# Full-precision array pieces for the attention's scores, the gate and z, and the first expert unit started after one sequence

## The chip, the cores and the metric

The kernel runs on one core of one Trainium2 chip. Its engines are TensorE (PE, with its weight loads shown as PEld), VectorE (DVE), ScalarE (ACT), GpSimd (POOL) and SyncE (SP, which issues the loads). Each works through its own queue in order. The metric is the device time of one execution in microseconds; the time of a kernel is the median of its runs.

## What is computed

Three networks follow one another (B = 4 sequences, 8 heads, 576 tokens, 64 columns a head, 32 packed keys; 2304 tokens of 512 columns in all):

```python
p_packed = sm_attn(p, k, v)                 # 32 packed queries against 576 keys, softmax
x = sm_attn(q, p_packed, p_packed)          # 576 queries against the 32 packed keys
P = exp(x @ w_gate - max)                   # 8 experts, then 8 rounds of row and column scaling
out = sum_e P[:, e] * (relu(x @ w1[e]) @ w2[e])       # w1: 512 x 1024, w2: 1024 x 512
h = relu(out @ w_in); y = (s * h * h + b) @ w_out     # 512 x 2048, 2048 x 512
```

All of it is float32. The large products are made of three products of rounded parts: high with high, high with low, low with high (`PASSES`), in the type fp32r. A product of two float32 tiles without such parts is called full precision here; the trace shows it as two instructions.

## The kernel before, in words

**The second attention is never multiplied by its values.** The experts read the weights of the second softmax instead (`xa`, heads x packed keys in 256 rows, high and low part), and the packed values are multiplied into w1: for each unit and pair of sequences, z = packed values x w1 (`zmm`, L340). A unit is 256 hidden columns of one expert; there are 32. Each unit goes over two pairs of sequences, a pair in four blocks of 288 tokens: `mm1a` (L373) multiplies z and xa, takes the relu on ACT (L381) and the residue on DVE (L382); `tile2` (L385) multiplies by w2 and `put1` (L394) adds to the sums of all tokens in `acc`, with the gate's factor `pm` from the fifth unit on.

**z before.** `zmm` makes four batches per unit (n = 0 to 3), each four fp32r matmuls over 128 rows that hold the high and low parts of two heads' values against w1's own high and low parts. w1 is loaded twice, into rows 0-63 and 64-127 (`load_w1`, L80), rounded on ACT (L88), and its residue made on POOL (L89). Since the values of four sequences stand side by side in 32-row blocks, `zput` (L355) takes a batch apart with six copies on ACT (L369) and six residues on DVE (L371).

**The attention before** goes in eight groups of four heads. The first scores (`s1`, L161) and the second ones (`s2`, L223) are full-precision matmuls on 64 columns of the array with zeros for the head that isn't meant (L167, L232); the values (`av`, L195) use 32 columns. A group goes through eleven stages, each a number of waves after its first (`STAGES`, L264; `wave`, L267), so several groups are under way. All eleven waves up to L522 are issued before the first `mm1a`; the remaining stages of the last groups run beside the four blocks of unit 0's first pair (L525 to L531).

**The order is written out by hand.** A block is a `slot` (L449): two `mm1a`, and between and behind them the `tile2` that earlier blocks made ready, each followed by one side job. `side1` (L479) gives the side jobs of the experts: one z batch at a time for the next unit, the loads of w1 and w2. From the second pair of unit 0 on each block also takes one step of `balance` (L273): the gate's products, then eight rounds of scaling (L320 to L335), each of a row part on DVE, one matmul with ones (L327) and a column part on DVE. It has 20 steps and is emptied after the first block of unit 3 (L549), ahead of the first use of `pm`.

**Buffers.** PSUM holds three banks for `tile2` (ps_y), two for `mm1a` (ps_h), three for all else (ps_m). Keys, values and first weights of the attention lie in `acc`, which the experts reach later. Loads are issued by SP in program order.

Of the kernel before, what the change touches and what calls it, by code (L numbers as in the profile page):

```python
# [30 lines left out]
KC, NKC = 96, 6      # keys of a chunk, chunks  # L31
SCALE = 1.0 / 8.0    # 1 / sqrt(HD)
# [5 lines left out]
def tile_kernel(ctx: ExitStack, tc: tile.TileContext, qT, kT, vv, pb, w1c, w2c, wcat64, wg, sv, bv, out):  # L38
# [20 lines left out]
    wgr = const.tile([128, NC, E], F32, name="wgr")  # L59
# [8 lines left out]

    def x_part(n, c):
        return xa[n][:, c, :] if c < 2 else xb[n][:, c - 2, :]  # L70

# [1 line left out]
    wts = {}  # L73
    tmp_p = []
# [5 lines left out]
    def load_w1(u):  # L80
        # a head's rows: high parts in rows 0-63, low parts in rows 64-127
        w = w_new((1, u))
        for i in range(2):
            r = raw_p.tile([128, 1024], F32, tag="raw", name="raw")
            for n in range(2):
                nc.sync.dma_start(out=r[64 * n:64 * n + 64, :], in_=w1c[u, :, 1024 * i:1024 * i + 1024])
            yield
            A.copy(w[:, i, :], r)  # L88
            G.tensor_tensor(out=w[64:128, i, :], in0=r[64:128, :], in1=w[64:128, i, :].bitcast(F32),  # L89
                            op=ALU.subtract)  # L90
# [9 lines left out]
    def load_w64(key, f):  # L100
        # float64 words to float32: (mantissa + 2^20) * (sign, exponent - 20), rounded to nearest
# [26 lines left out]
    NG = B * 2  # L128
    at = {}

# [3 lines left out]
    accf = acc.rearrange("p t d -> p (t d)")  # L134

    def spare(o, n):
        # rows of acc, which the experts reach after the attention
        return accf[:, o:o + n]

    def a_load(g):  # L140
        b, i = divmod(g, 2)
        if i == 0:
            pbs[b] = at_p.tile([128, NC, 2 * NPK], F32, tag="pbs", bufs=2, name="pbs")
            nc.sync.dma_start(out=pbs[b], in_=pb[:, b])
        k_ = spare(2 * S * (g % 3), 2 * S).rearrange("p (j t) -> p j t", j=2)
        nc.sync.dma_start(out=k_, in_=kT[b, :, 2 * i:2 * i + 2, :])
        at[g] = {"k": k_}

    def a_loadv(g):
        b, i = divmod(g, 2)  # L150
        v_ = spare(8 * S + NKC * 256 * (g % 2), NKC * 256)[:KC].rearrange("p (c m) -> p c m", c=NKC)
        nc.sync.dma_start(out=v_, in_=vv[b, :, :, 256 * i:256 * i + 256])
        at[g]["v"] = v_

    def a_loadq(g):
        b, i = divmod(g, 2)
        q_ = at_p.tile([128, 2, S], F32, tag="q", bufs=2, name="q_")
        nc.sync.dma_start(out=q_, in_=qT[b, :, 2 * i:2 * i + 2, :])
        at[g]["q"] = q_

    def s1(g):  # L161
        b, i = divmod(g, 2)
        k_, st = at[g].pop("k"), at_p.tile([128, 8], F32, tag="st", bufs=4, name="st")
        ps = [psa("y", "ps_s") for _ in range(2)]
        for hh in range(2):
            for j in range(2):
                mmul(ps[hh][64 * j:64 * j + 64, :HB], pbs[b][:, 2 * i + j, :],  # L167
                     k_[:, j, hh * HB:(hh + 1) * HB], start=True, stop=True)
            V.tensor_reduce(out=st[:, hh:hh + 1], in_=ps[hh][:, :HB], axis=AX.X, op=ALU.max)
        V.tensor_scalar(out=st[:, 2:3], in0=st[:, 0:1], scalar1=st[:, 1:2], scalar2=-SCALE,  # L170
                        op0=ALU.max, op1=ALU.mult)
        at[g]["st"], at[g]["s1"] = st, ps

    def exp1(g):
        st, ps, a1 = at[g]["st"], at[g].pop("s1"), spare(S * (6 + g % 2), S)
        for hh in range(2):
            A.activation(out=a1[:, hh * HB:(hh + 1) * HB], in_=ps[hh][:, :HB], func=AF.Exp,
                         bias=st[:, 2:3], scale=SCALE, accum_out=st[:, 3 + hh:4 + hh])
        V.tensor_scalar(out=st[:, 5:6], in0=st[:, 3:4], scalar1=st[:, 4:5], scalar2=EPS,
                        op0=ALU.add, op1=ALU.add)  # L180
        V.reciprocal(out=st[:, 6:7], in_=st[:, 5:6])
        at[g]["a1"] = a1

    def a1t(g):
        a1 = at[g].pop("a1")
        aT = at_p.tile([KC, NKC, 128], F32, tag="aT", bufs=2, name="aT")
        for hh in range(2):
            p_ = psa("m", "ps_t")
# [4 lines left out]
        at[g]["aT"] = aT  # L193

    def av(g):  # L195
        aT, v_, st = at[g].pop("aT"), at[g].pop("v"), at[g].pop("st")
        p_ = psa("m", "ps_v")
        for c in range(NKC):
            for n in range(4):
                r = slice(32 * n, 32 * n + 32)  # L200
                mmul(p_[r, :HD], aT[:, c, r], v_[:, c, HD * n:HD * n + HD], start=(c == 0), stop=(c == NKC - 1))
        w = at_p.tile([128, 2, HD], F32, tag="xw", bufs=2, name="xw")
        i_ = p_[:, :HD].rearrange("p (a d) -> p a d", a=1).to_broadcast([128, 2, HD])
        A.activation(out=w, in_=i_, func=AF.Copy, scale=st[:, 6:7])
        at[g]["w"] = w

    def ppt(g):
        # a head's packed values, transposed, in rows 0-63 and again in rows 64-127
        b, i = divmod(g, 2)
        p_ = psa("h", "ps_p")  # L210
        nc.tensor.transpose(p_[:, :128], at[g].pop("w").rearrange("p a d -> p (a d)"), ident)
        pv = p_[:, :128].rearrange("p (c j n) -> p c j n", c=2, j=2)
        for j in range(2):
            r, o = slice(64 * j, 64 * j + 64), NPK * (j ^ (b & 1))
            A.copy(ppf[r, b, 2 * i:2 * i + 2, o:o + NPK], pv[r, :, j, :])
        s_ = [p_[:, NPK * n:NPK * n + NPK] for n in range(4)]
        o = [[pp[:, i, n, k, b ^ n, :] for n in range(4)] for k in range(2)]
        for n in range(4):
            A.copy(o[0][n], s_[n])  # L219
        for n in range(4):  # L220
            V.tensor_tensor(out=o[1][n], in0=s_[n], in1=o[0][n].bitcast(F32), op=ALU.subtract)

    def s2(g):  # L223
        b, i = divmod(g, 2)
        q_ = at[g].pop("q")
        s_ = at_p.tile([128, S // 32, 32], F32, tag="s2", bufs=3, name="s2")
        st = at_p.tile([128, 4, S // 32, 1], F32, tag="st2", bufs=4, name="st2")
        for hh in range(2):
            p_ = psa("yh"[hh], "ps_q")
            for j in range(2):  # L230
                o = 64 * (j ^ (b >> 1))
                mmul(p_[o:o + 64, :HB], ppf[:, b, 2 * i + j, :], q_[:, j, hh * HB:(hh + 1) * HB],  # L232
                     start=True, stop=True)
            V.transpose(out=s_[:, 9 * hh:9 * hh + 9, :].rearrange("p t m -> p (t m)"), in_=p_[:, :HB])
        V.tensor_reduce(out=st[:, 0, :, 0], in_=s_, axis=AX.X, op=ALU.max)
        at[g]["s2"], at[g]["st2"] = s_, st

    def sub2(g):
        s_, st = at[g]["s2"], at[g]["st2"]
        G.tensor_tensor(out=s_, in0=s_, in1=st[:, 0].to_broadcast([128, S // 32, 32]), op=ALU.subtract)  # L240

    def exp2(g):
        A.activation(out=at[g]["s2"], in_=at[g]["s2"], func=AF.Exp, scale=SCALE)

    def norm2(g):
# [109 lines left out]
    def zput(u, n, p_, prs=(0, 1)):  # L355
# [3 lines left out]
        for q in range(4):  # L359
            r, pr = slice(32 * q, 32 * q + 32), (q >> 1) ^ k  # L360
            if pr not in prs:
                continue
# [257 lines left out]
```

## Time and profile before

| | us |
|---|---|
| median of 3 runs | 1840.36 |
| lowest, highest | 1840.31, 1841.12 |
| the profiled execution: its span | 1839.9 |
| PE, DVE, ACT, POOL busy in it | 1761.9, 1399.3, 809.2, 410.1 |

The profile is of one execution. Its span runs from the first to the last instruction; the median stands 0.4 us above it. "Lnnn" is a line of the kernel before. A row of the timeline has its start, how long it lasted from the first to the last end, engine, line, operation, the tiles (out <- in), its shape and count; what is in brackets is idle time of the engine ahead of it and what ended it. Consecutive instructions of one line are merged, and the end of a matmul includes its way through the array, so the start of the next row is the better mark of where a group's work was over. A row of the stage windows gives busy time (and instructions) per engine in that stretch, the mean granted clock of TensorE as a share of 2.4 GHz, the DMA engines' busy share, and what they moved.

### The profile page before, as it was taken

The numbers are of one execution on the slowest core, as the hardware profiler recorded it, in microseconds if no ns is written. First come the engines' busy times: TensorE is split into PE (matmuls) and PEld (weight loads), VectorE is DVE, ScalarE is ACT, GpSimd is POOL, SyncE is SP. The second block draws the span as 40 slices with busy tenths as digits, with TensorE's granted clock in tenths as the row PEclk, the third lists the DMA queues.
The fourth block names the chain that finished last, engine by engine and source line by source line (L and its number), as shares of the span: only waits on it lengthen the run. The fifth ranks groups of instructions, "written<-read, shape, count | busy, mean of one in ns | idle before, by whom it ended". The sixth has DMA issues, their size and how long they took to land.

```text
span 1839.9 us, 26426 instructions
## 1 busy us (share of the span) xinstructions
PE 1761.9 (96%) x9797; PEld 1519.7 (83%) x9797; DVE 1399.3 (76%) x2828; ACT 809.2 (44%) x1845; POOL 410.1 (22%) x288
## 2 busy tenths in 40 slices
PE   5789999999999999999999999999999999999999
PEld 2478888888888888888888888888888978888888
DVE  2757978777777777777777787777999489888874
ACT  3574475445444444544444454444434422222222
POOL 2541112111112211111221111121112233333332
PEclk9799999999999999999999999999999999999999
DMA  9421111111111111111111111111011011111102
GB/s 247 131 58 46 35 36 49 44 35 35 46 35 35 56 37 35 35 46 35 35 58 35 35 35 46 35 35 58 24 35 46 12 35 46 47 35 35 35 12 103
DMA packets 30225, 88.23 MB, mean 48 GB/s; under 512 B 4240, under 2 KB 9360, under 8 KB 30096
## 3 DMA queue, kind: packets, MB, share of 16 engines
q1 hardware_dynamic: 30096, 86.54, 16.2%
q8 instruction: 77, 1.26, 0.3%
q14 instruction: 52, 0.43, 0.1%
HBM read 81.81 MB, written 4.72 MB: 47 GB/s over the span
## 4 chain that ended last, share of the span: by engine, by line
PE 63%; DVE 20%; ACT 6%; issue 5%; POOL 2%; DMA 2%; SPq 0%; ACTq 0%; POOLq 0%; DVEq 0%
PE ps L390 37%; PE ps L378 18%; DVE z L371 6%; ACT z L369 5%; PE ps L415 5%; PE ps_z L351 2%; DVE m L120 2%; DVE ex L114 2%; DVE acc L403 1%; POOL h L425 1%; DVE m L119 1%; DVE acc L432 1%; DVE g L422 1%; DVE ex L116 1%; DVE ex L111 1%
## 5 line engine op out<-in xcount | busy, mean ns | idle before, releaser
L390 PE MATMUL ps<-w,h 128*128 128x512 f32 x4320 | 1119.3, 396 | 33.8 <-ACT h L424 9.4
L390 PEld LDWEIGHTS ps<-w,h 128*128 128x128 f32 x4320 | 778.5, 188 | 200.9 <-DVE h L382 19.9
L378 PEld LDWEIGHTS ps<-xa,z 128*128 128x128 f32 x3072 | 465.4, 189 | 46.6 <-ACT z L369 3.4
L378 PE MATMUL ps<-xa,z 128*128 128x288 f32 x3072 | 495.9, 297 | 4.9 <-ACT z L369 3.0
L403 DVE SCALAR_TENSOR_TENSOR acc<-ps,pm,acc 128x512 f32<-128x512 f32 x504 | 374.1, 747 | 109.3 <-PE ps L390 107.9
L381 ACT ACTIVATE h<-ps 128x288 fp32r<-128x288 f32 x512 | 210.7, 411 | 555.8 <-PE ps L378 502.3
L371 DVE TENSOR_TENSOR z<-ps_z,z 32x256 fp32r<-32x256 f32 (+1 forms) x768 | 370.3, 506 | 39.3 <-ACT z L369 33.8
L382 DVE SCALAR_TENSOR_TENSOR h<-ps,h 128x288 fp32r<-128x288 f32 x512 | 232.6, 454 | 128.1 <-ACT h L381 121.3
L369 ACT CAST z<-ps_z 32x256 fp32r<-32x256 f32 (+1 forms) x768 | 310.2, 434 | 18.2 <-PE ps_z L351 7.2
L89 POOL TENSOR_TENSOR w<-raw,w 64x1024 fp32r<-64x1024 f32 x64 | 152.6, 2405 | 414.9 <-issue 378.7
L98 POOL TENSOR_TENSOR w<-raw,w 128x1024 fp32r<-128x1024 f32 x32 | 76.9, 2402 | 596.4 <-ACT w L97 560.2
L425 POOL TENSOR_TENSOR h<-g,h 128x384 fp32r<-128x384 f32 x96 | 100.9, 1051 | 249.2 <-ACT h L424 247.2
L415 PE MATMUL ps<-xa,w 128*128 128x384 f32 x576 | 147.5, 337 | 0.0
L415 PE MATMUL ps<-xb,w 128*128 128x384 f32 x576 | 147.1, 336 | 0.0
L424 ACT CAST h<-g 128x384 fp32r<-128x384 f32 x96 | 49.4, 514 | 161.2 <-DVE g L423 161.1
L422 DVE SCALAR_TENSOR_TENSOR g<-ps,r 128x384 f32<-128x384 f32 x96 | 53.0, 552 | 77.1 <-ACT r L421 75.7
L415 PEld LDWEIGHTS ps<-xa,w 128*128 128x128 f32 x576 | 105.6, 188 | 6.7
L415 PEld LDWEIGHTS ps<-xb,w 128*128 128x128 f32 x576 | 104.7, 188 | 0.0
L88 ACT CAST w<-raw 128x1024 fp32r<-128x1024 f32 x64 | 67.0, 1047 | 67.1 <-PE ps L390 63.0
L432 DVE TENSOR_TENSOR acc<-ps,acc 128x512 f32<-128x512 f32 x126 | 86.0, 684 | 9.2 <-PE ps L390 9.0
L351 PE MATMUL ps_z<-w,pp 128*128 128x256 f32 x512 | 82.4, 283 | 0.7 <-ACT pp L219 0.5
L124 POOL TENSOR_TENSOR w<-m,w 128x256 fp32r<-128x256 f32 x64 | 48.1, 751 | 127.0 <-ACT w L123 127.0
(108 smaller groups left out, 776.9 us busy)
## 6 DMA issues: line engine op xcount, KB each, us to landing
raw<-w1c SPq DMA_DIRECT2D x128, 256.0 KB, 3.9
raw<-w2c SPq DMA_DIRECT2D x32, 512.0 KB, 3.4
raw<-wcat SPq DMA_DIRECT2D x32, 512.0 KB, 3.4
acc<-kT SPq DMA_DIRECT2D x8, 576.0 KB, 9.6
acc<-vv SPq DMA_DIRECT2D x8, 576.0 KB, 10.5
out<-acc SPq DMA_DIRECT2D x18, 256.0 KB, 2.0
q__224<-qT SPq DMA_DIRECT2D x1, 576.0 KB, 10.2
q__299<-qT SPq DMA_DIRECT2D x1, 576.0 KB, 14.8
```

What stands on the lines that cost most here:

```text
L89: G.tensor_tensor(out=w[64:128, i, :], in0=r[64:128, :], in1=w[64:128, i, :].bitcast(F32), op=ALU.subtract)
L351: mmul(p_[:, j * FU:(j + 1) * FU], pp[:, i, m, a].rearrange("p q n -> p (q n)"), w[:, (4 * i + m) * FU:(4 * i + m + 1) * FU], start=(a == ...
L369: A.copy(o[:, 0], i_)
L371: V.tensor_tensor(out=o[:, 1], in0=i_, in1=o[:, 0].bitcast(F32), op=ALU.subtract)
L378: mmul(p_[:, :HB], z[:, a, q // 2, i, f * 128:(f + 1) * 128], xa[k][:, i, t], start=(n + i == 0), stop=(n + i == 3))
L381: A.activation(out=hh, in_=p_[:, :HB], func=AF.Relu)
L382: V.scalar_tensor_tensor(out=hl, in0=p_[:, :HB], scalar=0.0, in1=hh.bitcast(F32), op0=ALU.max, op1=ALU.subtract)
L390: mmul(y, h[:, f, a, hc:hc + 128], ws[f][k], start=(n == 0), stop=(n == 3 * UF - 1))
L403: V.scalar_tensor_tensor(out=a, in0=y, scalar=pm[:, T, u // UE:u // UE + 1], in1=a, op0=ALU.mult, op1=ALU.add)
L415: mmul(p, w[:, a, c * 128:(c + 1) * 128], x_part(k, c)[:, b * BLK:(b + 1) * BLK], start=(n == 0), stop=(n == 3 * NC - 1))
L425: G.tensor_tensor(out=hl, in0=g, in1=hh.bitcast(F32), op=ALU.subtract)
L432: V.tensor_tensor(out=a, in0=y, in1=a, op=ALU.add)
```

## The change

Scores, gate and z become full-precision matmuls on pieces of 64 rows and 32 columns of the array, one piece a head, eight heads at a time. `heads()` names the piece of a head: row half r, column quarter c. Two PSUM banks, one for each row half, take the results.

- z: one job per unit and pair of sequences, 16 matmuls of 256 columns, then per bank one copy on ACT and one residue on DVE over 128 rows. w1 is loaded once, as it is; there is no rounding and no residue of it.
- Packed values stay in one layout (`ppf`); the zero blocks and the rounded copies go.
- The attention goes by sequence. The first runs alone up to its `xa`, with its subtractions and products on DVE; the next one's scores and exponentials follow. Then unit 0 begins: two blocks for each sequence, the next sequence's attention as their side jobs. From the third block on, in the first block of a sequence, the `tile2` go ahead of the `mm1a` (`behind`).
- `slot` spreads many side jobs over the block instead of one per job and the rest at the end.
- The gate's steps begin with unit 1 and are emptied where they were.
- w1 is loaded some one and a half units ahead. PSUM: ps_y 2, ps_h 2, ps_m 4. z has three buffers instead of four.

```diff
-    z_p = pool("z", 4)
-    ps_y = pool("ps_y", 3, space=bass.MemoryType.PSUM)
+    z_p = pool("z", 3)
+    ps_y = pool("ps_y", 2, space=bass.MemoryType.PSUM)
...
-    ps_m = pool("ps_m", 3, space=bass.MemoryType.PSUM)
+    ps_m = pool("ps_m", 4, space=bass.MemoryType.PSUM)
...
+    def heads():
+        for c in range(4):
+            for r in range(2):
+                yield r, c, slice(64 * r, 64 * r + 64), slice(32 * c, 32 * c + 32)
...
     def load_w1(u):
...
+        w = wts[1, u] = w1_p[-1].tile([128, 4, FU], F32, tag="w1", name="w1_")
+        wv = w1c[u].rearrange("d (c r m) -> r d c m", c=4, r=2)
+        for r in range(2):
+            nc.sync.dma_start(out=w[64 * r:64 * r + 64], in_=wv[r])
...
+    def s1(b, hh, tags="mm"):
+        ps = [psa(t, "ps_s") for t in tags]
+        for r, c, rows, cols in heads():
+            mmul(ps[r][cols, :HB], pbs[rows, b, c, NPK * r:NPK * r + NPK],
+                 at["k", b, c // 2][rows, c % 2, hh * HB:(hh + 1) * HB], start=True, stop=True)
+        at["s1", b, hh] = ps
...
+    def ppt(b, tag="m"):
+        p_ = psa(tag, "ps_p")
+        nc.tensor.transpose(p_[:, :128], at.pop(("w", b)).rearrange("p r d -> p (r d)"), ident)
+        A.copy(ppf[:, b, :], p_[:, :128])
...
+    def s2(b, hh, tags="mm"):
+        ps = at["s2p", b, hh] = [psa(t, "ps_q") for t in tags]
+        for r, c, rows, cols in heads():
+            mmul(ps[r][cols, :HB], ppf[rows, b, cols],
+                 at["q", b, c // 2][rows, c % 2, hh * HB:(hh + 1) * HB], start=True, stop=True)
...
+    def zmm(u, pr, qs=(0, 1)):
+        w = wts[1, u]
+        ps = [psm("ps_z") for _ in range(2)]
+        for q in qs:
+            for r, c, rows, cols in heads():
+                mmul(ps[r][cols, q * FU:(q + 1) * FU], ppf[rows, 2 * pr + q, cols], w[rows, c, :],
+                     start=True, stop=True)
+        return ps
+
+    def zput(u, pr, ps, qs=(0, 1)):
...
+        for r in range(2):
+            i_ = ps[r].rearrange("p (q m) -> p q m", q=2)[:, qs[0]:qs[-1] + 1]
+            A.copy(z[:, 0, qs[0]:qs[-1] + 1, r, :], i_)
+            V.tensor_tensor(out=z[:, 1, qs[0]:qs[-1] + 1, r, :], in0=i_,
+                            in1=z[:, 0, qs[0]:qs[-1] + 1, r, :].bitcast(F32), op=ALU.subtract)
...
-    def slot(first, side=()):
+    def slot(first, side=(), behind=False):
...
-        per = [first[0]] + todo[:1] + [first[1]] + todo[1:]
+        per = todo + first if behind else [first[0]] + todo[:1] + [first[1]] + todo[1:]
+        done = 0
         for n, job in enumerate(per):
             job()
-            if side:
-                side.pop(0)()
-        for s_ in side:
+            upto = max(min(n + 1, len(side)), len(side) * (n + 1) // len(per))
+            while done < upto:
+                side[done]()
+                done += 1
+        for s_ in side[done:]:
             s_()
...
     def side1(x, q):
         jobs = []
+        u, pr = order[x]
+        if u + 1 < U1 and (pr, q) in ((0, 2), (1, 0)):
+            jobs.append(zjob(u + 1, pr))
+        if (pr, q) == (1, 1) and u + 2 < U1:
+            jobs.append(lambda: load_w1(u + 2))
+        if (pr, q) == (0, 1) and u >= 1 and u + 1 < U1:
+            jobs.append(lambda: list(load_w2(u + 1)))
         return jobs
...
+            def block(s):
+
+                n, j = s + 1, []
+                if n < B:
+                    j += [lambda: a1t(n, 0), lambda: a1t(n, 1), lambda: (av(n, 0), av(n, 1)), lambda: ppt(n),
+                          lambda: s2(n, 0), lambda: (t2(n, 0), s2(n, 1)),
+                          lambda: (t2(n, 1), max2(n, 0, G)),
+                          lambda: (max2(n, 1, G), zput(0, n // 2, zmm(0, n // 2, (n % 2,)), (n % 2,))),
+                          lambda: exp2(n, 0)]
+                if n + 1 < B:
+                    j += [lambda: (s1(n + 1, 0), max1(n + 1, 0), s1(n + 1, 1), max1(n + 1, 1))]
+                if n < B:
+                    j += [lambda: (exp2(n, 1), norm2(n, 0, G))]
+                if n + 1 < B:
+                    j += [lambda: (exp1(n + 1, 0), den1(n + 1, 0))]
+                if n < B:
+                    j += [lambda: (norm2(n, 1, G), a2x(n, 0, G))]
+                if n + 1 < B:
+                    j += [lambda: (exp1(n + 1, 1), den1(n + 1, 1))]
+                if n < B:
+                    j += [lambda: a2x(n, 1, G)]
+                return j
...
+            for s in range(B):
+                for job in loads[s]:
+                    job()
+                jobs = block(s)
+                x, q = divmod(2 * s, 4)
+                k = (len(jobs) + 1) // 2
+                if s == 3:
+                    jobs, k = [zjob(1, 0), zjob(1, 1)], 1
+                slot1(x, q, jobs[:k], behind=s > 0)
+                slot1(x, q + 1, jobs[k:])
...
-            for x in range(1, len(order) - 1):
+            for x in range(2, len(order) - 1):
```

In `block`, t2 is the DVE transposes of the second scores, max2 their maximum (DVE) and its subtraction, norm2 the sum and reciprocal (DVE) and the product, a2x the transposes, the rounding (ACT) and the residue; the subtraction, the product and the residue are POOL's (G) here and DVE's (V) for the first sequence.

## Rows read from the trace of the kernel before

**Rows 1.** Part 1 of the page, all engines.
```profile
PE 1761.9 (96%) x9797; PEld 1519.7 (83%) x9797; DVE 1399.3 (76%) x2828; ACT 809.2 (44%) x1845; POOL 410.1 (22%) x288
```

**Rows 2.** Stage windows of the whole kernel: PE, PEld, DVE, ACT, POOL, PEclk, DMA, GB/s.
```profile
0.00:78.00 78.00, 45.99 (x576) 25.89 (x576) 36.20 (x115) 36.24 (x125) 27.98 (x26) 0.87 0.85 223
78.00:110.00 32.00, 22.04 (x121) 16.91 (x121) 25.44 (x56) 23.14 (x51) 13.94 (x10) 0.78 0.12 34
...
600.00:800.00 200.00, 198.80 (x1094) 173.24 (x1094) 154.44 (x290) 95.87 (x215) 34.91 (x16) 1.00 0.14 40
```

**Rows 3.** Timeline of PE, from the start to unit 1's first block.
```profile
5.84 2.19 PE L167 MATMUL ps_s<-acc,pbs 128*64 128x288 f32 x8 [5.84 <-DMA acc<-kT]
...
78.23 0.40 PE L378 MATMUL ps<-xa,z 128*128 128x288 f32 x1 [0.89 <-ACT z L369]
...
110.02 1.65 PE L390 MATMUL ps<-w,h 128*128 128x512 f32 x3 [4.12 <-ACT h L381]
...
135.73 0.56 PE L378 MATMUL ps<-xa,z 128*128 128x288 f32 x3
```

**Rows 4.** Part 5 of the page: the residues of z on DVE.
```profile
L371 DVE TENSOR_TENSOR z<-ps_z,z 32x256 fp32r<-32x256 f32 (+1 forms) x768 | 370.3, 506 | 39.3 <-ACT z L369 33.8
```

**Rows 5.** Timeline of PE, a steady unit; 715.82 answers to 675.63.
```profile
675.63 1.55 PE L390 MATMUL ps<-w,h 128*128 128x512 f32 x6
677.02 0.95 PE L378 MATMUL ps<-xa,z 128*128 128x288 f32 x6
677.81 1.54 PE L390 MATMUL ps<-w,h 128*128 128x512 f32 x6
...
684.80 0.63 PE L351 MATMUL ps_z<-w,pp 128*128 128x256 f32 x4
685.27 1.84 PE L390 MATMUL ps<-w,h 128*128 128x512 f32 x6
...
715.82 1.55 PE L390 MATMUL ps<-w,h 128*128 128x512 f32 x6
```

**Rows 6.** Timeline of PE: a full-precision matmul of full width in the gate.
```profile
178.35 0.51 PE L327 MATMUL ps_k<-pm,ones 128*128 128x144 f32 x2
178.61 1.05 PE L378 MATMUL ps<-xa,z 128*128 128x288 f32 x6
```

**Rows 7.** Timeline of PE: full-precision matmuls on column slices, clock at 2.4 GHz.
```profile
20.62 0.94 PE L201 MATMUL ps_v<-acc,aT 96*32 96x64 f32 x48
21.48 1.19 PE L167 MATMUL ps_s<-acc,pbs 128*64 128x288 f32 x8
22.61 0.86 PE L191 MATMUL ps_t<-ident,acc 128*96 128x128 f32 x6
```

**Rows 8.** Instructions by line and shape: busy us, mean ns, idle before.
```profile
L177 ACT ACTIVATE acc<-ps_s,st 128x288 f32<-128x288 f32 x16 | 7.9, 500 | 6.7 <-DVE st L170 6.6
L234 DVE STREAM_TRANSPOSE s<-ps_q 128x288 f32<-128x288 f32 x16 | 7.1, 470 | 10.6 <-PE ps_q L232 10.1
L192 ACT COPY aT<-ps_t 96x384 f32<-96x384 f32 x16 | 7.1, 482 | 12.4 <-PE ps_t L191 12.4
L235 DVE TENSOR_REDUCE st<-s 128x18 f32<-128x576 f32 x8 | 6.0, 753 | 0.3
L254 DVE STREAM_TRANSPOSE a2T<-s 128x576 f32<-128x576 f32 x8 | 5.9, 732 | 0.0
L250 POOL TENSOR_TENSOR s<-s,st 128x576 f32<-128x576 f32 x8 | 9.3, 1159 | 17.3 <-DVE st L249 17.3
L261 POOL TENSOR_TENSOR xa<-a2T,xa 128x576 fp32r<-128x576 f32 x8 | 11.3, 1415 | 6.2 <-ACT xa L260 6.1
```

**Rows 9.** Windows of the gate's rounds on DVE: tile skr (six rounds), tile skc (five).
```profile
174.00:215.00 41.00, 6.21 (x24) 1.00 0.14 40
...
174.00:215.00 41.00, 7.13 (x20) 1.00 0.14 40
```

**Rows 10.** Timeline of the second network: PE's two tiles, DVE's addition before.
```profile
1531.99 2.92 PE L390 MATMUL ps<-w,h 128*128 128x512 f32 x12
...
1533.11 0.68 DVE L432 TENSOR_TENSOR acc<-ps,acc 128x512 f32<-128x512 f32 x1
```

More of the change, by code (lines that the diff above doesn't have):

```diff
@@ L125, in load_w64 @@
                 yield
-    NG = B * 2
     at = {}
+    accf = acc.rearrange("p t d -> p (t d)")
     def psa(tag, name):
         return {"m": ps_m, "y": ps_y, "h": ps_h}[tag].tile([128, 512], F32, tag=tag, name=name)
[L134 to L164, printed above, removed]
-        for hh in range(2):
[L166 to L177, printed above, removed]
+    def spare(i, n):
+        return accf[:, 1536 * i:1536 * i + n]
+    def a_loadk(b, homes):
+        for i in range(2):
+            k_ = spare(homes[i], 2 * S).rearrange("p (c t) -> p c t", c=2)
+            nc.sync.dma_start(out=k_, in_=kT[b, :, 2 * i:2 * i + 2, :])
+            at["k", b, i] = k_
@@ new lines, in a_loadv, with a_loadq @@
+    def a_loadv(b, homes):
+        for i in range(2):
+            if homes[i] is None:
+                v_ = w_p.tile([128, 2048], F32, tag="w", name="v_")[:, :NKC * 256]
+            else:
+                v_ = spare(homes[i], NKC * 256)
+            v_ = v_[:KC].rearrange("p (n m) -> p n m", n=NKC)
+            nc.sync.dma_start(out=v_, in_=vv[b, :, :, 256 * i:256 * i + 256])
+            at["v", b, i] = v_
+    def a_loadq(b):
+        for i in range(2):
+            q_ = at_p.tile([128, 2, S], F32, tag="q", bufs=4, name="q_")
+            nc.sync.dma_start(out=q_, in_=qT[b, :, 2 * i:2 * i + 2, :])
+            at["q", b, i] = q_
@@ L207, in ppt @@
[L207 to L221, printed above, removed]
@@ L238, in sub2, with av @@
[L238 to L245, printed above, removed]
-        s_, st = at[g]["s2"], at[g].pop("st2")
+    def av(b, r, tag="m"):
+        aT, st = at.pop(("aT", b, r)), at.pop(("st", b, r))
+        p_ = psa(tag, "ps_v")
+        for cc in range(NKC):
+            for c in range(4):
+                o = slice(32 * c, 32 * c + 32)
+                m = HD * (2 * (c % 2) + r)
+                mmul(p_[o, :HD], aT[:, cc, o], at["v", b, c // 2][:, cc, m:m + HD],
+                     start=(cc == 0), stop=(cc == NKC - 1))
+        if r == 0:
+            at["w", b] = at_p.tile([128, 2, HD], F32, tag="xw", bufs=2, name="xw")
+        A.activation(out=at["w", b][:, r, :], in_=p_[:, :HD], func=AF.Copy, scale=st[:, 6:7])
@@ new lines, in ppt, with t2 @@
+    def ppt(b, tag="m"):
[7 more added lines that the diff above has]
+                 at["q", b, c // 2][rows, c % 2, hh * HB:(hh + 1) * HB], start=True, stop=True)
+    def t2(b, hh):
+        ps = at.pop(("s2p", b, hh))
+        for r in range(2):
+            if hh == 0:
+                at["s2", b, r] = at_p.tile([128, S // 32, 32], F32, tag="s2", bufs=2, name="s2")
+            o = at["s2", b, r][:, 9 * hh:9 * hh + 9, :]
+            V.transpose(out=o.rearrange("p t m -> p (t m)"), in_=ps[r][:, :HB])
@@ L462, in slot, with slot1 @@
         del coming[:]
[L464 removed]
+    def slot1(x, q, side=(), behind=False):
         u, pr = order[x]
@@ L469, in slot1 @@
             coming.append(lambda t=t: tile2(ws, t * 128, pr * 9 + t, put1(u)))
-        slot(first, side)
+        slot(first, side, behind)
     def slot2(v, b, side=()):
@@ L522, in tile_kernel @@
[L522 to L532 removed]
+            a_loadk(1, (2, 5))
@@ new lines, in tile_kernel @@
+            for hh in range(2):
+                s1(0, hh)
+                max1(0, hh)
+            a_loadv(1, (None, 1))
+            w20 = load_w2(0)
+            next(w20)
+            a_loadq(1)
+            for r in range(2):
+                exp1(0, r)
+                den1(0, r)
+            for r in range(2):
+                a1t(0, r, ("yy", "hh")[r])
+            for r in range(2):
+                av(0, r)
+            a_loadk(2, (3, 4))
+            ppt(0)
+            for hh in range(2):
+                s2(0, hh)
+                t2(0, hh)
@@ new lines, in tile_kernel @@
+            zp = zmm(0, 0, (0,))
+            for r in range(2):
+                max2(0, r, V)
+                exp2(0, r)
+            for r in range(2):
+                norm2(0, r, V)
+                if r == 0:
+                    zput(0, 0, zp, (0,))
+                a2x(0, r, V)
+            for hh in range(2):
+                s1(1, hh)
+                max1(1, hh)
+            next(w20, None)
+            for r in range(2):
+                exp1(1, r)
+                den1(1, r)
+            def block(s):
[19 more added lines that the diff above has]
+                return j
```

202 lines of the change are left out of this document (65 added, 137 removed).

## The prediction, made before the changed kernel had run

> **What bounds the kernel now.** I read the page first. TensorE (PE) is busy for 96% of the span [rows 1], so only its idle time and the length of its own work can be won. The stage windows say where the idle time lies [rows 2]. In the middle of the experts PE is busy for 198.8 of 200 us. In the first 78 us it is busy for 46.0, in the next 32 us for 22.0, there at a mean granted clock of 0.78. So the middle is PE's own work, and the head waits on other engines and on loads.
>
> The timeline of PE dates the head [rows 3]. The first scores start when the first keys land, at 5.84 us. The first product of the experts starts at 78.23, when all four sequences have their attention nearly done. Unit 1 of the experts, its first block, starts at 135.73. Unit 0 thus takes 57.5 us, where a steady unit takes 715.82 - 675.63 = 40.2 [rows 5]. The page's list of costly groups shows what z costs off PE: its rounding residues alone are 768 DVE instructions and 370 us of DVE [rows 4].
>
> **The change, part by part.** Everything is summed against the profiled span, 1839.9 us (0.4 below the median of the runs, 1840.36). I split it at the start of unit 1: 135.7 before, 1704.2 after.
>
> *z of a steady unit.* Before: four batches of four full-width matmuls, 0.47 us each (684.80 to 685.27) [rows 5], so 1.9. Behind the second batch six matmuls of L390 take 1.84 us busy instead of 1.55, because ACT and DVE are held by the many small copies: 0.3. The 1.2 us that PE idles in 200 [rows 2] are 0.24 per unit. Together 2.45. After: two jobs of 16 full-precision matmuls on 64x32 pieces of the array, two instructions each. A full-precision instruction makes two passes: two of 144 columns take 0.26 us at full width (178.35 to 178.61) [rows 6], which is 2 x 144 columns at 2.4 GHz each. So one of 256 columns takes 0.213, and 32 of them 6.8 us one behind another. How many run at once is not in this trace for halves of the rows; it is for slices of the columns [rows 7]. Eight instructions of 288 columns on two 64-column slices (L167) would take 1.92 in a row, and the next work starts after 1.13 (21.48 to 22.61). 48 instructions of 64 columns on four 32-column slices (L201) would take 2.56, and the next work starts after 0.86. Less the streaming (0.96 and 0.64) both leave about 0.2, the price of going to another shape. So as many run at once as there are disjoint pieces. The bounds for a job are therefore 6.8 / 8 + 0.2 = 1.05 and, with only the column slices at once, 6.8 / 4 + 0.2 = 1.9. I take 1.1, near the lower end, because row halves are as disjoint as column slices, and the two halves write different PSUM banks. A unit then pays 2.2 instead of 2.45: 31 units x -0.25 = **-8**. The DVE and ACT relief, and POOL's w1 residues that vanish, are costed at nothing beyond this: PE's own work hides them.
>
> *The head.* The first scores need all of pbs and both halves of the keys, 1664 KB instead of 704. At the 223 GB/s of the first window [rows 2] that is 4.4 us later than 5.84: 10. From there the first sequence runs alone. I add up durations [rows 8], on engines that work in order. Scores at half clock and the last two maxima (taken as the 0.47 of a transpose of that shape, L234): 13.4. Exponentials of two sets of four heads (0.5 twice each, and their sums read out), the first weights following at once: 16. Four copies of transposed weights (0.48): 18. Values, their transpose and copies: 21.3. Second scores and four DVE transposes (0.47): 24.4. Twice a maximum (0.75) and a subtraction, on DVE here, about as long (0.7): 27.3. Then on DVE twice a normalisation (a sum of 0.75, two small ones of some 0.25, a product of 0.7) and a transpose (0.73), with z's two residues and the copies between: 36. The next sequence's maxima and exponentials follow in the same queues, ahead of ACT's relu of the first block: **41**. Loads keep ahead: by the tiles' sizes sequence 1's queries end 8.7 MB into the queue, 39 us at that rate, and are wanted at 46.
>
> Each further sequence then passes beside two blocks of unit 0. PE has about 16 us for both: four L378 groups at 0.8, 4.5 tiles at 1.39 [rows 5], and 6.5 of attention and z. The chain is longer. From the end of one sequence's last ACT copy to the next one's: four ACT copies 1.9, an accumulator copy 0.6 (L192's 0.48, from 384 to 512 columns), values 0.9 and their scaling 0.4, transpose and copy 0.6, second scores 0.65; then DVE: four transposes 1.9, two maxima 1.5, residues of z and h 1.7, the next sequence's maxima 2.2, two normalisations 2.5, a wait for POOL's multiplication 1.16, a transpose 0.73; and an ACT copy 0.67. This is 17.4. Hand-overs between engines and PE partly at half clock make it 20, my estimate. The third sequence has no successor: 17.5. After it POOL's last residue (1.41), two blocks of 4.7 less the tiles already done, and two z jobs: 8.5. So unit 1 starts at 41 + 20 + 20 + 17.5 + 8.5 + 2 for stalls I cannot place = **109** instead of 135.7.
>
> Here a rule is weighed. In 78 to 110 PE was busy 22 of 32 us and got 0.78 of its clock [rows 2]. At that share 16 us of PE work take 20 and the period holds. The Trainium skill, page TensorE: Matmul & The Clock Gate, section Part 1: The HAM clock gate, says that half rate is the default and that activity releases it; a head that never earned it would take some 27 us of PE per sequence (an estimate from the page's two rates), and the sum would be 1838 instead of 1816. I go by the row.
>
> *The gate.* It starts one half-unit later relative to the units: its small products and half of its 32 products of 288 columns (0.13 each, L378's pace [rows 5]) move behind unit 1's start: +3. Sixteen blocks are left for its 20 steps before the experts' scaling needs them, plus one; so two Sinkhorn iterations and the last scaling run at the end of a block with nothing between. An iteration is 1.04 + 1.43 us of DVE [rows 9] (6.21 / 6 and 7.13 / 5), behind DVE's last tile (some 0.7, by the addition of the same size [rows 10]), and PE stands for both: 0.7 + 2 x (2.47 + 0.26) = **+6**.
>
> *PSUM.* The y buffers fall from three to two. In the second network the third tile of a block starts 1.39 after 1531.99, at 1533.38, while DVE's addition of the first ends at 1533.11 + 0.68 = 1533.79 [rows 10]. With two buffers it would wait 0.4. Some 17 tiles look like this: at most 7. The first tile of the next block waits for h anyway, which hides most: **+2** (0 to 7). In the experts DVE has room after z shrinks: 0. The w1 loads halve in bytes and lie in front of SP's queue by a unit and a half: 0.
>
> Sum: 109 + 1704.2 - 8 + 3 + 6 + 2 = 1816.2; with 0.4 outside the span, 1816.
>
> **The rivals.** *Halves one after the other* (slower). Only the column slices of the array run at once. Then a z job costs 1.9, 62 jobs x 0.8 = +50, and the scores in the head add 6: 1872. It decides from 1.5 us per job on, where 62 x 0.39 eats the gain of 24. For it: no row shows two row halves. Against it: both column shapes ran at full width. Chance 0.12.
>
> *The head stays slow.* PE falls to half clock between its bursts, or ACT and DVE queue behind each other as at 110.02, where PE waited 4.1 us for one relu [rows 3]. A mean clock of 0.6 makes PE's 16 us 25 to 26: unit 1 starts at 125, total 1832. For it: 0.78 is a mean over full and half rate. Against it: the blocks of unit 0 now fill the gaps that the waves left. Chance 0.14.
>
> *PE sets the head.* The chain's parts overlap more than I lay them, the period is PE's 16, unit 1 starts at 97, and a z job costs its lower bound: 12 and 3 less, 1801. Chance 0.12.
>
> **The numbers.** The forecast holds 0.62: 1816, with its own spread 1801 to 1831 (the period by 3 us, thrice; a z job by 0.1, 62 times). About 0.2% is what a measurement of this kernel can tell from no change, so 1837 is the border. Faster: 0.62 + 0.12 + most of the slow head = 0.83. Same 0.05. Slower 0.12. The range 1797 to 1838 takes in the slow and the fast head and leaves out the row halves, and little else.
>
> **What would show it.** PE's timeline: first experts' product at 36 to 37, unit 1's first block near 109, blocks of unit 0 some 20 us apart in pairs. z: 32 instructions of 64x32 within 1.1 us, steady units 39.9 to 40.0 apart. PE idle twice for about 3 us at the gate's L327 in the fourth unit. If a z job takes 1.9, or unit 1 starts past 130, the forecast is wrong.

## The result, and the profile after

The changed kernel takes 1809.45 us (median of 4 runs, 1807.71 to 1810.38) where the kernel before took 1840.34 beside it (4 runs): ratio 0.9828, 95% interval 0.9814 to 0.9842, so 31 us faster. The forecast was 1816, 24 us faster. The profiled execution took 1809.04 us, its span is 1807.2, 32.7 shorter than the profiled span before. Line numbers in the rows below are those of each run's own kernel.

Part 1 of the page of the kernel after, the answer to [rows 1], and from part 5 the z residues that answer to [rows 4]:

```profile
PE 1751.6 (97%) x11489; PEld 1486.4 (82%) x11489; DVE 1144.8 (63%) x2167; ACT 499.8 (28%) x1102; POOL 248.7 (14%) x217
...
L347 DVE TENSOR_TENSOR z<-ps_z,z 128x512 fp32r<-128x512 f32 (+1 forms) x132 | 82.9, 670 | 50.0 <-ACT z L346 50.0
```

The residues of z fell from 768 instructions and 370 us of DVE to 132 and 83. ACT lost 309 us of work and POOL 161. PE lost only 10, and it is PE that sets the time: the span is PE's work and PE's gaps.

The stage windows of the kernel after, with the columns of [rows 2]:

```profile
0.00:36.00 36.00, 17.86 (x233) 9.85 (x234) 16.66 (x41) 12.20 (x32) 3.05 (x7) 0.82 1.02 287
36.00:56.00 20.00, 16.98 (x236) 12.51 (x235) 11.26 (x32) 9.73 (x28) 6.00 (x5) 0.89 0.96 227
56.00:76.00 20.00, 16.67 (x235) 11.58 (x234) 10.31 (x31) 11.09 (x29) 7.42 (x6) 1.00 0.40 127
76.00:95.00 19.00, 16.80 (x240) 11.92 (x237) 9.25 (x20) 9.70 (x22) 6.62 (x6) 1.00 0.13 29
95.00:110.00 15.00, 11.76 (x137) 9.03 (x137) 5.19 (x9) 9.46 (x17) 10.29 (x6) 0.77 0.34 99
600.00:800.00 200.00, 200.00 (x1343) 170.21 (x1343) 116.38 (x191) 48.44 (x105) 12.01 (x5) 1.00 0.10 27
```

From 36 to 95 us PE is now busy for 50.5 of 59 us, at a clock of 0.89 and then 1.00. In the middle of the experts its last idle 1.2 us of 200 are gone.

PE's timeline in the head, the answer to [rows 3], and behind it the kernel before at unit 1's first tile:

```profile
5.99 1.18 PE L168 MATMUL ps_s<-acc,pbs 64*32 64x288 f32 x8 [5.99 <-DMA acc<-kT]
...
27.38 0.61 PE L355 MATMUL ps<-xa,z 128*128 128x288 f32 x1 [0.18 <-ACT xa L259]
31.65 1.57 PE L355 MATMUL ps<-xa,z 128*128 128x288 f32 x5 [3.67 <-ACT xa L259]
...
46.52 1.20 PE L168 MATMUL ps_s<-acc,pbs 64*32 64x288 f32 x32
47.65 1.06 PE L355 MATMUL ps<-xa,z 128*128 128x288 f32 x6
...
108.52 0.95 PE L355 MATMUL ps<-xa,z 128*128 128x288 f32 x6
...
115.86 1.32 PE L367 MATMUL ps<-w,h 128*128 128x512 f32 x5
```

```profile
143.78 1.55 PE L390 MATMUL ps<-w,h 128*128 128x512 f32 x6
```

Unit 0's first product starts at 27.4 instead of 78.2, and unit 1's first block at 108.5 instead of 135.7. The last line of the first fence is unit 1's first tile, at 115.9 instead of 143.8. So the head gives 27.9 us of the 32.7.

PE's timeline around a z job of a steady unit, the answer to [rows 5], with the same job of the next unit:

```profile
611.92 0.95 PE L355 MATMUL ps<-xa,z 128*128 128x288 f32 x6
612.80 1.09 PE L336 MATMUL ps_z<-w__5451,ppf 64*32 64x256 f32 x32
613.82 1.65 PE L367 MATMUL ps<-w,h 128*128 128x512 f32 x6
615.31 0.95 PE L355 MATMUL ps<-xa,z 128*128 128x288 f32 x6
...
652.76 1.09 PE L336 MATMUL ps_z<-w__5793,ppf 64*32 64x256 f32 x32
```

32 instructions of 256 columns, 6.8 us one behind another, take 1.02 us: all eight pieces work at once. The total alone would also fit instructions of one pass, four at a time; the single starts in this trace do not. Eight instructions start between 612.80 and 612.85, the next eights at 613.04, 613.26 and 613.47, so from the second on an eight takes 0.215 us, two passes of 256 columns at 2.4 GHz. The group ahead takes 0.88 (0.80 elsewhere), the tile behind 1.49 (1.39), so the job costs PE 1.2. The unit is 652.76 - 612.80 = 39.96 us long; before, 40.19.

### The profile page after: what moved, and what is told of

The parts are those of the page before. It is cut to its first block, busy times and chain, and to the rows that moved or that the text cites. A ratio compares the mean times of both kernels' runs of the same rounds, so it can differ in the third digit from the quotient of the medians.

```text
span 1807.2 us, 28193 instructions
## 1 busy us (share of the span) xinstructions
PE 1751.6 (97%) x11489; PEld 1486.4 (82%) x11489; DVE 1144.8 (63%) x2167; ACT 499.8 (28%) x1102; POOL 248.7 (14%) x217
## 3 DMA queue, kind: packets, MB, share of 16 engines
q8 instruction: 91, 1.49, 0.4%
## 4 chain that ended last, share of the span: by engine, by line
issue 57%; PE 22%; DVE 15%; POOL 5%; ACT 1%; DMA 1%; SPq 0%; POOLq 0%; ACTq 0%; DVEq 0%
PE ps L367 11%; PE ps L392 5%; POOL w L102 4%; PE ps L355 3%; DVE ex L118 2%; DVE m L124 2%; DVE acc L409 2%; DVE m L123 1%; DVE g L399 1%; DVE ex L120 1%; DVE ex L115 1%; DVE ex L117 1%; DVE g L400 1%; DVE raw L122 1%; POOL h L402 1%
## 5 line engine op out<-in xcount | busy, mean ns | idle before, releaser
L367 PE MATMUL ps<-w,h 128*128 128x512 f32 x4320 | 1109.0, 395 | 22.8 <-DVE acc L409 14.5
L347 DVE TENSOR_TENSOR z<-ps_z,z 128x512 fp32r<-128x512 f32 (+1 forms) x132 | 82.9, 670 | 50.0 <-ACT z L346 50.0
L399 DVE SCALAR_TENSOR_TENSOR g<-ps,r 128x384 f32<-128x384 f32 x96 | 53.1, 553 | 78.2 <-ACT r L398 78.2
L346 ACT CAST z<-ps_z 128x512 fp32r<-128x512 f32 (+1 forms) x132 | 69.2, 576 | 39.8 <-PE ps_z L336 39.6
L398 ACT ACTIVATE r<-ps 128x384 f32<-128x384 f32 x96 | 46.9, 489 | 61.1 <-PE ps L392 60.6
L127 ACT CAST w<-m 128x256 fp32r<-128x256 f32 x64 | 26.0, 407 | 92.7 <-DVE m L124 85.1
L101 ACT CAST w<-raw 128x1024 fp32r<-128x1024 f32 x32 | 33.6, 1051 | 63.9 <-PE ps L367 61.5
```

The lines of the kernel that those rows point to most:

```text
L346: A.copy(z[:, 0, qs[0]:qs[-1] + 1, r, :], i_)
L347: V.tensor_tensor(out=z[:, 1, qs[0]:qs[-1] + 1, r, :], in0=i_, in1=z[:, 0, qs[0]:qs[-1] + 1, r, :].bitcast(F32), op=ALU.subtract)
L367: mmul(y, h[:, f, a, hc:hc + 128], ws[f][k], start=(n == 0), stop=(n == 3 * UF - 1))
L399: V.scalar_tensor_tensor(out=g, in0=p, scalar=0.0, in1=r, op0=ALU.max, op1=ALU.mult)
```

## The experiments

The theory after the result: (a) the head's gain is the overlap of attention with unit 0's blocks; (b) a z job is streaming on eight pieces at once plus a price for going to another shape and back; (c) what is left in the head stands in the order of the engines' queues. The first four runs tell (a) and (b) from their rivals; the kernel before took 1843.30 beside them.

**Attention first.** All attention is issued ahead of unit 0's blocks:

```diff
             for s in range(B):
                 for job in loads[s]:
                     job()
-                jobs = block(s)
+                for job in block(s):
+                    job()
+            for s in range(B):
+                jobs = []
```

> All of the attention is issued ahead of unit 0's eight blocks, which then run with no attention beside them; nothing else changes. Theory (the head's gain is the overlap): a sequence alone needs about 17 us instead of 20, so the last weights are ready at 36 + 3 x 17 + 1.4 = 89, and the eight blocks follow at PE's pace (16 half blocks of 0.8, 15 tiles of 1.39, two z jobs: 36). Unit 1 starts at 125 instead of 108.5: 1809 + 16 = 1825. Rival (the gain came from the cheaper attention alone, the blocks beside it are worth little): unit 1 starts within 5 us of 108.5, 1809 to 1814.

1832.82 us (ratio to before 0.9940, 0.9923 to 0.9957), 23 more than the changed kernel. Its windows in the head:

```profile
36.00:56.00 20.00, 13.92 (x201) 8.24 (x199) 10.39 (x30) 8.42 (x26) 5.99 (x5) 0.59 0.78 203
56.00:76.00 20.00, 11.57 (x193) 6.66 (x192) 10.12 (x27) 8.94 (x24) 7.76 (x7) 0.59 0.45 139
```

and PE's timeline where attention ends and the blocks begin:

```profile
83.27 2.99 PE L355 MATMUL ps<-xa,z 128*128 128x288 f32 x12
94.88 1.81 PE L355 MATMUL ps<-xa,z 128*128 128x288 f32 x6 [8.61 <-DVE h L359]
...
141.01 1.55 PE L367 MATMUL ps<-w,h 128*128 128x512 f32 x6
```

Unit 1's first tile (last line) is 25.2 us later than in the changed kernel. So without the blocks beside it the cheaper attention keeps 2.8 of the head's 27.9. By the ends of ACT's last rounding copies the three sequences take 19.9, 18.6 and 17.5 us instead of 20.6, 20.6 and 20.0, so the chain gains little from having the engines to itself; what is lost is the PE work that lay beside it. The first block's relu stands in ACT's queue behind all attention (the last rounding copy starts at 92.40), and PE waits 8.6 us for it. Theory (a) holds. The run costs 8 us more than I expected because the three sequences took 5 more than the 51 that I had put, the first of them ended 1 later, and the blocks took some 3 more than 36. PE had 0.59 of its clock beside the sequences; how much of the 8 us that explains is not shown.

**z twice.** Each job's matmuls are issued twice from unit 1 on:

```diff
-        for q in qs:
+        for q in list(qs) * (2 if u > 0 else 1):
```

> From unit 1 on every z job issues its 16 matmuls twice, the second time over the first results: 62 jobs get 32 more instructions of 256 columns, with no further change of the array's shape. Theory (eight pieces at once, on PE's path): 62 x 0.85 = +53, 1862. Rival (only the four column slices at once): 62 x 1.7 = +106, 1915. Rival (z is hidden behind something else): 1809.

1868.35 us (1.0136, 1.0120 to 1.0151), so 59 us more than the changed kernel. A unit is 41.73 us long, 1.77 more: 0.885 for each doubled job, or 55 for 62 of them; three of the experts' last five units grew by 5 more together, where PE's waits for DVE's additions rose from 2.3 to 6.0 and the granted clock was 0.50 from 1229 to 1232 us. PE's timeline:

```profile
634.83 1.96 PE L336 MATMUL ps_z<-w__5867,ppf 64*32 64x256 f32 x64
636.72 1.66 PE L367 MATMUL ps<-w,h 128*128 128x512 f32 x6
```

64 instructions take 1.89, against 1.02 for 32. The second half costs its streaming, 6.8 / 8 = 0.85, and hardly more.

**z in halves.** A job is split in two of half the size, in neighbouring blocks: the same streaming, twice as many changes of shape.

```diff
-        if u + 1 < U1 and (pr, q) in ((0, 2), (1, 0)):
-            jobs.append(zjob(u + 1, pr))
+        if u + 1 < U1 and (pr, q) in ((0, 2), (0, 3), (1, 0), (1, 1)):
+            k = (q % 2,)
+            jobs.append(lambda: zput(u + 1, pr, zmm(u + 1, pr, k), k))
```

> From unit 2 on each z job is cut in two of eight matmuls (one sequence each) in neighbouring blocks: as many matmuls, 60 more changes of the array's shape, and twice the copies on ACT and DVE at half the size. Theory (a job pays about 0.2 us for going to the small pieces and back): 60 x 0.2 to 0.25 = +12 to +15, 1821 to 1824. Rival (a change costs nothing, the 0.2 was the first matmul's way through the array): 1809 to 1811. Rival (a full drain of 0.4 or more): 1833 and up.

1827.01 us (0.9913, 0.9898 to 0.9928), above the 1821 to 1824 that I expected. A unit is 40.73 long, 0.77 more for two more jobs: 0.385 for one pair of changes, where 0.2 to 0.25 was expected. Sixty times that would be 23, and the kernel lost only some 18: the experts' last units are 40.73 long as well, so the waits that lengthen three of them in the changed kernel (41.22, 41.59 and 40.35) are gone, and the fourth unit even fell from 43.87 to 43.17 (for which see the gate early). PE's timeline around a half job:

```profile
630.73 0.95 PE L355 MATMUL ps<-xa,z 128*128 128x288 f32 x6
631.61 0.66 PE L336 MATMUL ps_z<-w__5603,ppf 64*32 64x256 f32 x16
632.20 1.66 PE L367 MATMUL ps<-w,h 128*128 128x512 f32 x6
633.70 0.95 PE L355 MATMUL ps<-xa,z 128*128 128x288 f32 x6
```

0.59 for the job, 0.08 ahead and 0.11 behind it, less 0.43 of streaming: 0.35. The price of a change does not shrink with the job. Theory (b) holds, at nearly twice the price that I read from [rows 7]: there I took a group from its own start to the next one's, which is 0.17 above streaming here too (1.02 less 0.85), and left out what the groups ahead and behind lose (0.08 and 0.10). The type of the numbers alone does not cost this: the gate's full-precision matmul of full width takes 0.26 for 0.24 of streaming [rows 6]. The Trainium skill, page TensorEngine Tiling (Array Packing), section Key Properties, says that a change of mode drains the engine; it gives no price, and this one agrees with it (the last eight instructions of a job start 0.35 ahead of the tile, not 0.215).

**Row halves in turn.** The order of issue puts all four pieces of the upper half ahead of the lower:

```diff
-        for c in range(4):
-            for r in range(2):
+        for r in range(2):
+            for c in range(4):
```

> The eight pieces are issued with the four column quarters of one row half first, then those of the other, instead of the two halves in turn; scores, gate and z all follow. Theory (pieces run at once because they are disjoint, whatever their order): 1809, within 2. Rival (the halves overlap only when issued in turn): a z job takes up to 0.85 longer, up to 1809 + 62 x 0.85 = 1862.

1808.45 us (0.9812, 0.9797 to 0.9827), units of 39.96 as before. The halves overlap in either order.

The next four went together; the kernel before took 1843.35 beside them. Their base is the changed kernel again: 1808.82 us (0.9814, 0.9794 to 0.9833).

> The changed kernel once more, as the base for the runs beside it: 1809, within 2.

**Three y buffers.** `ps_m` falls to three banks, and an eighth bank is the fourth of `ps_m` in the head and the third of `ps_y` from unit 1 on:

```diff
-    ps_m = pool("ps_m", 4, space=bass.MemoryType.PSUM)
+    ps_m = pool("ps_m", 3, space=bass.MemoryType.PSUM)
...
+            extra["m"] = psx
...
+            del extra["m"]
+        extra["y"] = ctx.enter_context(tc.tile_pool(name="psy3", bufs=1, space=bass.MemoryType.PSUM))
```

> From unit 1 on the second products have three PSUM banks again and the rest three instead of four (in the head two and four, as in the changed kernel). Theory (PE's 14.5 us of waits for DVE's additions in the second network took the place of its waits for h, which end at the same time): 0 to -3, 1806 to 1809. Rival (those waits are on the path): -10 to -14, 1795 to 1799.

1808.30 us (0.9808, 0.9787 to 0.9828), 0.5 below the base, which the medians can't tell from nothing; the profiled span is 1806.2 against 1808.5. PE's waits in the second network of the changed kernel (total, times, longest, all in us but the times):

```profile
PE ps L367 <- DVE acc L409: 12.2, 20, 1.0
PE ps L367 <- ACT h L401: 0.7, 3, 0.2
```

of the kernel before:

```profile
PE ps L390 <- ACT h L424: 9.4, 13, 0.8
PE ps L390 <- POOL h L425: 7.1, 18, 0.5
```

and of this one:

```profile
PE ps L375 <- ACT h L409: 8.4, 11, 1.1
PE ps L375 <- POOL h L410: 5.8, 15, 0.5
```

The wait for a free y buffer took the place of the wait for h, and a third buffer brings the old wait back: the forecast's cover was the right one. (Of the 14.5 us that I expected to find in the second network, 2.3 lie in the experts.) What the third buffer does save lies in the experts' last units (41.22, 41.59 and 40.35 become 40.51, 39.96 and 39.96), where the changed kernel has this wait of PE, and this one has none:

```profile
PE ps L367 <- DVE acc L380: 2.3, 4, 1.0
```

**The gate early.** Two steps of the gate go into each of the first four blocks, so that none is left to run at an end:

```diff
                     if bal is not None:
                         side.append(nxt(bal))
+                        if x == 2:
+                            side.append(nxt(bal))
```

> In the first four blocks of unit 1 the gate takes two steps instead of one, so that its twenty steps are done before the block where the rest is emptied; no work is added. Theory (the fourth unit's surplus of 3.9 us over a steady 39.96 is the emptied steps): -2 to -4, 1805 to 1807, the fourth unit at 40 to 41. Rival (the surplus is the gate's own work, which only moves): 1809.

1805.99 us (0.9801, 0.9782 to 0.9820), 2.8 below the base. The fourth unit falls from 43.87 to 39.96, the second grows by 1.1 and the third shrinks by 0.7: 3.5 in all in the profile. In the changed kernel the fourth unit holds this wait, which is gone, and behind it two groups at half clock:

```profile
209.79 0.48 PE L317 MATMUL ps_k<-pm,ones 128*128 128x144 f32 x2 [1.91 <-DVE pm L315]
...
210.81 1.58 PE L355 MATMUL ps<-xa,z 128*128 128x288 f32 x6
212.32 1.96 PE L336 MATMUL ps_z<-w__1936,ppf 64*32 64x256 f32 x32
214.21 1.65 PE L367 MATMUL ps<-w,h 128*128 128x512 f32 x6
```

The group takes 1.51 instead of 0.88 and the z job 1.89 instead of 1.02: the granted clock was 0.50 from 211 to 214 us. These two lose 1.5 us, and with the wait they make up 3.4 of the unit's surplus of 3.9. In this run the clock stays at 1.00 there (200 to 250 us). The fall does not always follow: in the run with z in halves the same wait of 1.9 stands there, the clock stays at 1.00 (205 to 250 us), and the fourth unit's surplus is 2.4.

**The next sequence's values early.** Its weight transposes and values are issued between the last steps of the present sequence:

```diff
-                    j += [lambda: (norm2(n, 1, G), a2x(n, 0, G))]
+                    j += [lambda: norm2(n, 1, G)]
...
+                if n < B:
+                    j += [lambda: a2x(n, 0, G)]
+                if n + 1 < B:
+                    j += [lambda: a1t(n + 1, 0)]
...
+                    j += [lambda: a2x(n, 1, G)]
+                if n + 1 < B:
+                    j += [lambda: (a1t(n + 1, 1), av(n + 1, 0), av(n + 1, 1))]
```

> In the head the next sequence's transposes and first values are issued between the last steps of the present one, instead of behind them in the next block. Theory (the 20 us per sequence are the order of ACT's and DVE's queues, with PE idle between): the period falls to about 17, unit 1 starts 4 to 8 us earlier, 1801 to 1805. Rival (PE's own work sets the period): 1808 to 1809. Rival (the weights of the present sequence come later by what is put before them): 1809 to 1813.

1812.51 us (0.9835, 0.9816 to 0.9854): slower by 3.7, and my expectation missed. PE's waits from 36 to 110 us of this kernel, first lines:

```profile
PE ps_v L213 <- ACT aT L204: 8.1, 4, 2.8
PE ps L355 <- ACT xa L259: 1.8, 1, 1.8
```

In the changed kernel the first of them is 0.8. The values now reach the head of PE's queue before ACT has copied their weights, and the experts' tiles behind them stand still. The time lies in the range of my second rival, and the weights did come later: the first rounding copies of the three sequences start 23.0 and 21.6 us apart, instead of 20.6 and 20.3. The idea had to be split: the copies may move on ACT, the values may not on PE.

**Copies first.** ACT's order changes: the next sequence's exponentials and its copies of transposed weights go ahead of the present sequence's rounding, and the values stay at the head of the next block. PE's transposes of these weights and DVE's small sums move along with them. The diff is that of the run before, with `av` left where it was and `a1t(n + 1, 0)` ahead of `a2x(n, 0, G)`. The kernel before took 1842.54 beside this run and the next two.

> As the run before with the next sequence's transposes early, but the exponentials of both sets and the copies of the transposed weights go ahead of the present sequence's rounding on ACT, and the values stay at the head of the next block, so that no values matmul stands at the head of PE's queue. Theory (ACT's order sets the period, and the run before lost its gain to PE's queue, where the values blocked the tiles behind them): the period falls from 20.4 to 17 or 18, unit 1 starts 3 to 6 us earlier, 1803 to 1806. Rival (PE's queue sets the period whatever ACT's order): 1808 to 1813.

1805.84 us (0.9799, 0.9785 to 0.9812). ACT's timeline in the changed kernel:

```profile
49.59 0.49 ACT L187 ACTIVATE a<-ps_s,st 128x288 f32<-128x288 f32 x1
...
52.76 0.67 ACT L259 CAST xa<-a2T 128x576 fp32r<-128x576 f32 x1 [2.59 <-DVE a2T L257]
...
53.81 0.51 ACT L187 ACTIVATE a<-ps_s,st 128x288 f32<-128x288 f32 x1
...
73.38 0.67 ACT L259 CAST xa<-a2T 128x576 fp32r<-128x576 f32 x1 [2.53 <-DVE a2T L257]
```

and in this one:

```profile
49.29 0.51 ACT L187 ACTIVATE a<-ps_s,st 128x288 f32<-128x288 f32 x1
...
52.21 0.68 ACT L259 CAST xa<-a2T 128x576 fp32r<-128x576 f32 x1 [0.52 <-DVE a2T L257]
...
71.16 0.68 ACT L259 CAST xa<-a2T 128x576 fp32r<-128x576 f32 x1 [0.58 <-DVE a2T L257]
```

and its unit 1's first tile on PE:

```profile
111.00 1.55 PE L367 MATMUL ps<-w,h 128*128 128x512 f32 x6
```

ACT no longer stands for 2.6 us before a rounding whose input is not there, with ready exponentials behind it. The third sequence's first rounding starts 18.95 us after the second's (73.38 - 52.76 = 20.6 in the changed kernel), and unit 1's first tile comes at 111.0 instead of 115.9. Theory (c) holds for this part of the queue's order; the period stayed above the 17 to 18 that I expected.

**Two and three together.** Copies first with the gate early, and both with the third y buffer:

> The run above and the gate's steps taken early. Theory (the two lie in different stretches, so they add): 3 less than the run above, 1800 to 1803.

> The run above with three PSUM banks for the second products from unit 1 on. Theory (they save the three single waits of units 27 to 30 and nothing in the second network): 1 to 3 less than the run above, 1798 to 1802.

1804.04 us (0.9788, 0.9774 to 0.9802), 1 above what was expected, and 1799.52 us (1797.72 to 1800.52; 0.9764, 0.9750 to 0.9777). The second is the fastest kernel here: 43 us below the kernel before and 9 to 10 below the changed one. In its profile the fourth unit is 39.96 long, and three of the experts' last units went from 41.22, 41.59 and 40.35 to 40.48, 39.96 and 39.96. The third buffer is worth 2.1 in the profiled spans here (1799.5 to 1797.4) and 2.3 alone; the medians, with 4.5 and 0.5, scatter about that.

## Why the prediction was right

The forecast's mechanism is what happened: the head gained by overlap, z by eight pieces at once. Several of its terms were off in either direction and partly cancelled; that the head came out within 0.5 us is luck in part. The head's steps are read from ACT's timeline: the exponentials end at 36.1, the last rounding copies of the next three sequences at 56.7, 77.3 and 97.3. In us:

| step | forecast | measured |
|---|---|---|
| first sequence, to its successor's exponentials | 41 | 36.1 |
| two periods beside blocks | 20, 20 | 20.6, 20.6 |
| last sequence | 17.5 | 20.0 |
| rest to unit 1 | 10.5 | 11.2 |
| unit 1's first block | 109 | 108.5 |
| z, each steady unit | -0.25 | -0.23 |
| gate, moved behind unit 1's start (units 1 and 2) | +3 | -0.1 |
| gate, emptied steps (unit 3) | +6 | +2.8 |
| z in the experts' units | -8 | -4.9 (units 4 to 31) |
| second network | +2 | -2.6 |

- **The head.** The first sequence was 5 us early. I let its scores wait for both halves of the keys, to 10 us; the first eight instructions start at 5.99 with one half, the others at 7.87, and the queue moved 287 GB/s in the first 36 us, where I had taken the 223 that are a mean of 78. That won 2.3 us up to the first exponentials (11.1 instead of 13.4); the rest came in small pieces behind them. The last sequence was 2.5 late: without a successor it still goes at the pace of ACT's waits for DVE (96.66, a wait of 2.3 before its rounding). The two errors left the sum within 0.5.
- **The period of 20** was 17.4 of chain and an allowance of 2.6 for hand-overs. The measured 20.6 makes it 3.2, and copies first shows what half of it was (20.6 to 18.95): an instruction in ACT's queue ahead of its input.
- **z.** I took 0.85 of streaming and 0.2 for the shape; the first is right, the second is 0.35, so a job costs 1.2 instead of 1.1. The steady unit still gained 0.23, so the old z cost 2.4 + 0.23 = 2.63, not the 2.45 I summed; where the other 0.2 lay is not shown. Over all units the gain is less than 8, because the experts' last five grew by 0.2 in sum: there PE waits for y buffers, which I had costed at nothing ("in the experts DVE has room").
- **The gate** was too dear. The second and third unit changed by +2.4 and -2.5 against before, so moving the work cost nothing net. Of the emptied steps all but one came between tiles that PE had ready; it waited once, for 1.9, not twice for 3, and lost another 1.5 at half clock behind it, for which I had no term.
- **The second network.** Of the buffers' 0 to 7 it took the lower end (+0.5 over seven of its units). What I had no term for is its first unit, which fell from 57.41 to 54.37: before, PE waited there as follows, and that wait is gone. In the run with three y buffers `ps_m` has three banks again, PE waits there for 0.9, and the unit takes 54.92; so the fourth bank is not what removed most of the wait, and what did is not shown.

```profile
PE ps_f L440 <- DVE xb L443: 3.2, 2, 2.7
```

From unit 1's first tile to the end the kernel became 4.8 us shorter (1696.1 to 1691.3), where the last four lines of the table had made it 3 longer. These 7.8 us, 0.5 of the head and 0.7 between unit 1's first block and first tile are the 9 us by which the span came out below 1816.2. Outside the span lay 1.8 us of the profiled execution, not 0.4, which brought the median nearer.

- **The rivals.** *Halves one after the other* falls with 1.02 for a job of 32 whose instructions start in eights, and again with the doubled jobs. *The head stays slow* falls with the clock at 0.89 and 1.00; attention first shows that the danger was real, for without the blocks beside it the same attention ran at 0.59. (The sums on it were off: 16 us of PE are 32 at half rate, not 27, and 26.7 at a clock of 0.6.) *PE sets the head* did not come about either: PE was busy for 17.0 and 16.7 us of two windows of 20. After copies first it is 17.8 of 20 in the second such window, which is where that rival begins.

## What to carry to other kernels

Where a chain over several engines has gaps, the gain of putting a ready engine's work beside it can be read off beforehand: sum the chain's durations, add a little for hand-overs, and check that PE's work fits inside; here that gave 109 for 108.5, from parts that were off by up to 5 us. Then look at each queue of the result for an instruction that stands ahead of its input with ready work behind it, and reorder one engine at a time, since the order that frees ACT blocked PE. Price matmuls on 64x32 pieces as streaming divided by the pieces plus 0.35 us for each visit, counted from the group ahead to the group behind, and make the visits few. A wait of PE can cost more than its length: look at the granted clock behind it.

## What the runs showed of the hardware

- Going to 64x32 full-precision pieces and back between full-width work costs 0.35 to 0.385 us, for 16, 32 or 64 instructions alike; eight pieces then stream at once (eight starts within 0.05 us, 0.215 from one eight to the next), in either order of the row halves (39.96 a unit in both).
- PE's granted clock does not follow its busy share alone: busy for 13.9 of 20 us (70%) it had 0.59 in the attention-first run, and busy for 22.0 of 32 (69%) it had 0.78 before [rows 2]. Both are means over stretches at half and at full rate (in the attention-first run 0.50 from 52 to 65 us and 1.00 from 66 to 68). With the blocks in the same gaps it had 0.89 at 17.0 of 20. The sequences at 0.59 took no longer than those at the higher clock with blocks beside them; what they would take alone at full rate no run shows.
- In the fourth unit of the changed kernel PE stood for 1.9 us in the middle of dense work, and the clock was 0.50 from 211 to 214 us; where the gate early takes that wait away, it stays at 1.00. In the run with z in halves the wait is there and the clock stays at 1.00 all the same.
